# One layout for two batches of x, and a first q in two pieces: attention into an FFN on one core

## The chip, the core and the metric

One core of a Trainium2 chip runs the whole program. The metric is the device time of one execution in microseconds (us). The kernel before took 543.62 us, the median of 8 runs that lie between 543.4 and 544.74.

## The reference

Attention with a squared relu instead of a softmax, for 8 batches of 12 heads, 448 tokens and a head width of 64; then a block with a normalization and two FFN layers on x, which has 448 tokens of 768 features.

```python
scores = scale * np.matmul(q, k.transpose(0, 1, 3, 2))
attn = np.maximum(scores, 0.0) ** 2 / S
x = np.matmul(attn, v)            # heads side by side: (8, 448, 768)
mu, var = mean and variance of x over its 768 features
xn = (x - mu) / np.sqrt(var + 1e-06) * g_ln
out = x + np.maximum(xn @ w_ch1, 0.0) @ w_ch2    # 768 -> 3072 -> 768
```

Inputs and output are fp32; the kernel computes in bf16 with fp32 sums.

## The kernel before

TensorE does everything that is a product. Per batch the 12 heads go in three groups (n counts them over all batches, `NPER = 3` per batch). For a group: q and k are turned (line 474 on TensorE for batches 0 and 1, a DMA transpose at line 405 for the others), `att_QK` makes scores for seven blocks s of 64 tokens (line 552), ACT or DVE applies the relu (561, 563), DVE, POOL or ACT squares (578, 576), and `att_AV` multiplies by v (616). Its result is x transposed: features on partitions, tokens along the row, six blocks `ki` of 128 features.

`att_AV` copies it out of PSUM (helper at 354 for ACT and 356 for DVE) into `xT_e` or `xT_o`, for even and odd batches, each three blocks of 128 tokens, and `xT_left`, which holds the remaining 64 tokens of an even and an odd batch side by side. So a copy has two parts, `reg` (384 tokens) and `left` (64). From there three things are made:

- the mean over features: for batch 0 `mean_part` (681, 683) multiplies by a matrix of 1/768; for later batches POOL adds first (`sum_part`, 706 to 709) and `center` (785, 789) multiplies the sum;
- the centred x: DVE subtracts the mean (826 and 829 for batches 0 and 1, 807 for others), then ACT, or DVE, multiplies by the gain (814, 816). This is the input of FFN layer 1 (876 for the first three columns of batch 0, 893 for the rest; evacuated with a relu at 909 and 911);
- x token by token, from which variance and residual come: `after_x` turns it by a DMA transpose that SP issues (729 for the three blocks, 741 for the left one), DVE takes the statistics (754 to 756), ACT and DVE make the reciprocal root (765, 767). FFN layer 2 (950) needs these only when its result is evacuated (964).

`load_first` brings the first group of batch 0 as fp32 by SP's queue (344) and has it cast (356); all other loads go by POOL's queue, which casts on the way (324, 376, 416, 422, 392), at most eight in flight.

The order of the instructions is made by a planner, `Order`, before anything runs. Each piece of work has an estimated cost; `R.add` puts it among those that wait, with the engines that may do it, and `best` takes the one that can start first, on the engine that would finish it first. TensorE's work is put in by `R.pe` in an order of its own: for batch 0 whichever of two streams (scores, and the rest) can start sooner, afterwards by `greedy` and `segment`. Every engine then runs its own list strictly in that order, and waits at an instruction until its inputs are there. The planner's times only set the order. A few lines of the loop for batch 0:

```python
qk_stream += [("T", NPER)] + qks(NPER, 0, 3)
...
tA, tQ = (start_of(piece_deps(*st[0])) if st else FAR for st in (av_stream, qk_stream))
...
st = av_stream if tA <= tQ + 50.0 else qk_stream
```

Of the kernel before, what the change touches and what calls it, by code (L numbers as in the profile page):

```python
# [40 lines left out]
class Order:  # L41

    LAT = {"PE": 240.0, "ACT": 90.0, "DVE": 90.0, "POOL": 90.0, "SP": 0.0}
# [105 lines left out]
    def pe(self, cost, emit, deps=(), mode="F"):  # L151

        if mode != self.mode:
            cost += 90.0
        self.mode = mode
        op = Op("PE", cost, emit, deps, 0.0)
        while True:
            r = self.ready(op)
            p = self.best()
            if r is not None:  # L160
                t0 = max(r, self.free["PE"])
                if p is None or p[3] > t0:
                    break
            assert p is not None, "no work left that could release TensorE"
            self.wait.remove(p[1])
            self.commit(p[1], p[2], p[3])
        self.commit(op, "PE", t0)
        return op
# [28 lines left out]
def kernel(  # L197
# [43 lines left out]
    x_pool = ctx.enter_context(tc.tile_pool(name="x", bufs=2))  # L241
    xh_pool = ctx.enter_context(tc.tile_pool(name="xh", bufs=1))
# [16 lines left out]
    xT_e = const_pool.tile([P, 3, K1, P], bf16)  # L259
    xT_o = const_pool.tile([P, 3, K1, P], bf16)  # L260
    xT_left = const_pool.tile([P, K1, P], bf16)
# [8 lines left out]

    def xT_of(b):

        t, off = (xT_e, T) if b % 2 == 0 else (xT_o, 0)
        return t, xT_left[:, :, off:off + T]
# [3 lines left out]
    stage, vt, qkT, xT, xc, xm, mvs, rstd = {}, {}, {}, {}, {}, {}, {}, {}  # L278
# [49 lines left out]
    FIRST = ((0, 0, J), (1, 0, 3), (1, 3, J))  # L328

    def load_first():  # L330
# [3 lines left out]
        for i, (t, j0, j1) in enumerate(FIRST):  # L334
# [10 lines left out]
            ld = R.add("SP", 480.0, emit, [], key=float(i), load=(2 * P, (75.0, 43.0, 110.0)[i]))  # L345
# [119 lines left out]
    def att_T(n, part=0):  # L465
# [17 lines left out]
        if b == 0:  # L483
            evs = ops.setdefault(("T", n), [])
            pieces = list(enumerate(FIRST if n == 0 else ((0, 0, J), (1, 0, J))))
            for i, (t, j0, j1) in pieces[2 * part:2 * part + 2]:
# [37 lines left out]
    def qk_dep(n, s):  # L524
        b, pn = divmod(n, NPER)
        if ("T", n) in ops:
            if n == 0 and s >= FIRST[1][2]:
                return ops["T", n] if len(ops["T", n]) > 2 else None
            return ops["T", n][:2]
        if ("turn", b, 0) in ops:  # L530
            return [ops["turn", b, 0], ops["turn", b, 1]]
        return None

    def att_QK(n, s):
# [29 lines left out]
        late = FAR if n == 0 and s < FIRST[1][2] else 0.0 if s == 1 and n >= 2 * NPER else 600.0  # L564
# [35 lines left out]
    def att_AV(n, s):  # L600
# [24 lines left out]
        t, t_left = xT_of(b)  # L625

        free = ops.get(("x_read", b - 2), []) + ops.get(("turn_x", b - 2), [])
        if b % 2 == 0:
            free = free + ops.get(("turn_x", b - 1), [])
        evs = []  # L630
        if b == 0:
            for half in range(2):
                def evac(eng, half=half):
                    ki = pn + half * NPER
                    copy(eng, t[:, 0:3, ki, :], av_st[n][half][:, reg(b)].rearrange("p (m c) -> p m c", c=P))
                    copy(eng, t_left[:, ki, :], av_st[n][half][:, left(b)])
                ev = R.add(("DVE", "ACT"), (770.0, 760.0), evac, [op], key=-1.0)
                f_use(ev)
                evs.append(ev)
        else:  # L640
            def evac(eng, rest):
                ps = av_st[n, 1]
                if rest:
                    copy(eng, t_left[:, pn::NPER, :], ps[:, :, left(b)])
                else:
                    copy(eng, t[:, 0:3, pn::NPER, :].rearrange("p m h c -> p h m c"),
                         ps[:, :, reg(b)].rearrange("p h (m c) -> p h m c", c=P))
            ev0 = R.add(("DVE", "ACT"), (960.0, 800.0), lambda eng: evac(eng, False), [op] + free, key=-1.0)
            ev = R.add(("DVE", "ACT"), (295.0, 270.0), lambda eng: evac(eng, True), [op, ev0], key=-1.0)
            slot_use(ev)  # L650
            evs = [ev0, ev]
# [15 lines left out]
    def mean_part(n):  # L667
# [4 lines left out]
        def emit(eng):  # L672
# [5 lines left out]
            t, t_left = xT_of(b)  # L678
            for ki in (pn, pn + NPER):
                first, last = ki == 0, ki == K1 - 1  # L680
                nc.tensor.matmul(mean_ps[b][:, reg(b)], ones, t[:, 0:3, ki, :], start=first, stop=last,  # L681
                                 skip_group_check=True)
                nc.tensor.matmul(mean_ps[b][:, left(b)], ones, t_left[:, ki, :], start=False, stop=last,
                                 skip_group_check=True)
# [8 lines left out]
    def sum_part(n):  # L693

        b, pn = divmod(n, NPER)
        t, t_left = xT_of(b)

        def add(eng, rest):
            if rest:
                x0, x1 = t_left[:, pn, :], t_left[:, pn + NPER, :]  # L700
                s0, r_t = sum_t[:, left(b)], rsum_t[:, left(b)]
            else:
                x0, x1 = t[:, 0:3, pn, :], t[:, 0:3, pn + NPER, :]
                s0, r_t = (a[:, reg(b)].rearrange("p (m c) -> p m c", c=P) for a in (sum_t, rsum_t))
            if pn == 0:
                nc.gpsimd.tensor_add(s0, x0, x1)  # L706
            else:
                nc.gpsimd.tensor_add(s0, s0, x0)  # L708
                nc.gpsimd.tensor_add(s0 if pn < SUMMED[b] - 1 else r_t, s0, x1)
        k = 1 if pn == 0 else 2  # L710
        free = ops["x_read", b - 1] if pn == 0 else [ops["sum", n - 1]]
        a0 = R.add("POOL", 900.0 * k, lambda eng: add(eng, False), ops["x", n] + free, key=-2.0, port=True)
        ops["sum", n] = R.add("POOL", 250.0 * k, lambda eng: add(eng, True), [a0], key=-2.0,
                              port=True)
# [3 lines left out]
    def after_x(b):  # L718
# [4 lines left out]
        m0 = 0 if even else 4  # L723

        def turn(eng):
            a = x_pool.tile([P, 3, d_model], bf16, tag="x")
            for i in range(3):
                xm[u, m0 + i] = a[:, i, :]
            nc.sync.dma_start_transpose(
                a.rearrange("p m (k c) -> p (m k) c", c=P),  # L730
                xT_of(b)[0].rearrange("p m k c -> p (m k c)"))
        late = [ops["w1", K2 - 1]] if b == 0 else []
        tr = R.add("SP", 100.0, turn, xs + late + [ops.get(("f2_out", b - 2))], key=0.0, load=(3 * K1 * P, 18.0))

        deps_of = {m0 + i: tr for i in range(3)}
        ops["turn_x", b] = [tr]
        if not even:
            def turn_left(eng):
                a = xh_pool.tile([P, d_model], bf16, tag="xl")
                xm[u, 3] = a  # L740
                nc.sync.dma_start_transpose(
                    a.rearrange("p (k c) -> p k c", c=P), xT_left.rearrange("p k c -> p (k c)"))
            deps_of[3] = R.add("SP", 100.0, turn_left, xs + [ops.get(("m3_out", u - 1))],
                               key=0.0, load=(K1 * P, 18.0))
            ops["turn_x", b].append(deps_of[3])
        for m in sorted(deps_of):
            def stats(eng, m=m):
                if m == min(deps_of):
# [9 lines left out]
            if m == min(deps_of):  # L758
                ops["st0", b] = sto
            ops["st", u, m] = sto  # L760
        n_m = 3 if even else 4
        s0 = 0 if even else 3
# [3 lines left out]
        sq = R.add("ACT", 300.0, root, [ops["st", u, s0 + i] for i in range(n_m)], key=3.0)  # L766
# [6 lines left out]
    def center(b):  # L773

        st = {}
        t, t_left = xT_of(b)
        if b == 0:
            op = ops["mean", b]
        else:
            n_s = SUMMED[b]  # L780

            def emit(eng):
# [4 lines left out]
                for ki in rest:  # L787
                    for cols, i in ((reg(b), t[:, 0:3, ki, :]), (left(b), t_left[:, ki, :])):
                        nc.tensor.matmul(ps[:, cols], ones, i, start=False, stop=ki == rest[-1],
                                         skip_group_check=True)  # L790
# [29 lines left out]
        if b < 2:  # L820
            for ki in [pn + NPER * h for pn in range(NPER) for h in range(2)]:
                def sub_k(eng, ki=ki):
                    if ki == 0:
                        alloc()
                    mean = mean_ps[b]
                    nc.vector.tensor_sub(
                        xc[b][:, ki, reg(b)].rearrange("p (m c) -> p m c", c=P), t[:, 0:3, ki, :],
                        mean[:, reg(b)].rearrange("p (m c) -> p m c", c=P))
                    nc.vector.tensor_sub(xc[b][:, ki, left(b)], t_left[:, ki, :], mean[:, left(b)])
                s1 = R.add("DVE", 675.0, sub_k, [op], key=-2.0)  # L830
                subs.append(s1)
                c_ops.append(R.add(*GAIN_ON, lambda eng, ki=ki: gain(eng, ki), [s1], key=-2.5, port=True))
        else:
            for m in range(4):
# [25 lines left out]
    def ffn_1_first(b):  # L860
# [3 lines left out]
        def fill(eng):  # L864
# [5 lines left out]
            for i in range(N_FILL):  # L870
                nc.tensor.matmul(st[i % 2][0][:, :3 * P], ones, xT_e[:, :, 0, :], start=True, stop=True)
# [120 lines left out]
    def piece_deps(kind, n, *s):  # L992
# [3 lines left out]
        if kind == "T" and s:  # L996
            return [ops["qk_ld", 0, 0][2]]
# [152 lines left out]
    with tc.manual_schedule():  # L1150
# [28 lines left out]
        qk_stream += [("T", NPER)] + qks(NPER, 0, 3)  # L1179
# [20 lines left out]
        qk = [p for p in qk if p in qk_stream or p not in [("T", NPER)] + qks(NPER, 0, 3)]  # L1200
# [51 lines left out]
```

## Time and profile before

| | |
|---|---|
| median of 8 runs | 543.62 us |
| the profiled execution, its own time | 543.69 us |
| its span in the profile | 541.7 us |
| TensorE (PE) busy | 527.5 us, 97% |
| DVE, ACT, POOL busy | 286.2, 229.2, 113.5 us |
| chain that ended last, share of PE | 94% |
| first matmul, first FFN matmul | 5.01, 29.97 us |

The span is what the profiler recorded from the first to the last instruction; what lies around it is 2.0 us here. Busy is the time in which an engine had an instruction under way; TensorE's matmuls overlap, so a busy TensorE need not be at its peak. "Waits" are put down to what came last before an engine went on. In the chain each step is followed back to what released it. Durations of one instruction include its latency: two that follow each other on DVE or ACT overlap by some 0.08 to 0.1 us.

### The profile page before, as it was taken

Reading aid. Unit: us, or ns where it says so; the run is one execution under the profiler, and the core shown is the slowest. Engines: PE = TensorE matmul, PEld = TensorE weight load, DVE = VectorE, ACT = ScalarE, POOL = GpSimd, SP = SyncE. Lnnn points to the kernel's source line nnn. Section 1 sums busy time; section 2 is a strip of 40 time slices with the busy share of each in tenths; the row PEclk is TensorE's granted clock in tenths of the full one; section 3 lists DMA queues with packets and bytes.
Section 4 is the critical chain, followed back from the end, with each engine's and each line's share of the span. In section 5 each row is a group of like instructions: output and inputs, shape, how many; then the busy total and the mean of one; then the engine's idle time right before and its main releaser. Section 6 shows DMA issues by size and latency. Waiting matters only on the chain.

```text
span 541.7 us, 9897 instructions
## 1 busy us (share of the span) xinstructions
PE 527.5 (97%) x4208; PEld 285.7 (53%) x4208; DVE 286.2 (53%) x503; ACT 229.2 (42%) x380; POOL 113.5 (21%) x132
## 2 busy tenths in 40 slices
PE   4899999999999999999999999999999999999996
PEld 3444455555554455545555455555555545555553
DVE  5979557337774566735366446752556534530011
ACT  5977612124335642556125653265413654134200
POOL 6411700121350124311061121610220102100000
PEclk9999999999999999999999999999999999999999
DMA  9999999997299005970199502990032100510022
GB/s 195 205 198 185 209 162 169 155 137 136 69 157 181 7 1 94 194 114 2 31 108 204 75 1 55 161 187 1 1 68 66 30 0 1 111 36 1 1 58 60
DMA packets 141112, 51.83 MB, mean 96 GB/s; under 512 B 120966, under 2 KB 136844, under 8 KB 141068
## 3 DMA queue, kind: packets, MB, share of 16 engines
q0 software_dynamic: 81072, 25.50, 43.2%
q1 hardware_dynamic: 55516, 14.88, 18.4%
q10 hardware_dynamic: 4480, 10.82, 7.2%
q8 instruction: 33, 0.54, 0.4%
q14 instruction: 11, 0.09, 0.1%
HBM read 51.91 MB, written 11.01 MB: 116 GB/s over the span
## 4 chain that ended last, share of the span: by engine, by line
PE 94%; DVE 2%; DMA 1%; ACT 1%; issue 0%; POOL 0%; POOLq 0%; ACTq 0%; DVEq 0%
PE o_ps L950 41%; PE ps L893 40%; PE sc L552 6%; PE ps L616 5%; DMA t<-in_k_dram 1%; DVE a L578 1%; PE ps L876 1%; ACT a L561 1%; PE ps L474 0%; DVE t L356 0%; PE slot L785 0%; PE ps L681 0%; DVE a L563 0%; ACT a L576 0%; POOL t L324 0%
## 5 line engine op out<-in xcount | busy, mean ns | idle before, releaser
L893 PE MATMUL ps<-a,w 128*128 128x448 bf16 x1134 | 220.4, 353 | 0.0
L950 PE MATMUL o_ps<-w,h 128*128 128x384 bf16 x1200 | 199.7, 326 | 0.0
L893 PEld LDWEIGHTS <-w 128*128 128x128 bf16 x1134 | 108.3, 98 | 108.3 <-issue 10.8
L950 PEld LDWEIGHTS <-h 128*128 128x128 bf16 x1200 | 116.1, 98 | 81.5 <-issue 5.5
L909 ACT ACTIVATE h<-ps 128x448 bf16<-128x448 f32 (+1 forms) x162 | 85.5, 528 | 104.3 <-PE ps L893 103.3
L561 ACT ACTIVATE a<-sc 128x896 bf16<-128x896 f32 x102 | 90.4, 921 | 85.5 <-PE sc L552 81.2
L563 DVE TENSOR_SCALAR a<-sc 128x896 bf16<-128x896 f32 x57 | 62.0, 1087 | 103.4 <-PE sc L552 103.2
L578 DVE TENSOR_TENSOR a<-a 128x896 bf16<-128x896 bf16 x158 | 99.5, 667 | 3.4 <-ACT a L561 3.3
L964 DVE SCALAR_TENSOR_TENSOR o_t<-o_ps,r_t,a 128x384 f32<-128x384 f32 x56 | 34.4, 615 | 107.2 <-PE o_ps L950 106.8
L552 PE MATMUL sc<-t 64*64 64x448 bf16 x672 | 47.8, 361 | 2.0 <-ACT a L561 1.3
L616 PE MATMUL ps<-a,v_t 64*64 64x448 bf16 x636 | 37.0, 351 | 1.5 <-DVE a L578 0.5
L814 ACT ACTIVATE a<-a,g_sb 128x448 bf16<-128x448 bf16 x39 | 23.0, 657 | 26.0 <-DVE a L807 24.9
L552 PEld LDWEIGHTS <-t 64*64 64x64 bf16 x672 | 17.5, 106 | 23.6 <-issue 18.2
L616 PEld LDWEIGHTS <-v_t 64*64 64x64 bf16 x672 | 20.2, 107 | 16.8 <-issue 5.7
L392 POOL DMA_DIRECT2D t<-in_q_dram x12 | 19.3, 1773 | 27.2 <-DMA t<-t 25.7
L708 POOL TENSOR_TENSOR sum_t<-sum_t,xT_o 128x384 f32<-128x384 f32 x7 | 6.4, 914 | 85.4 <-ACT xT_o L354 72.3
L950 PE MATMUL o_ps<-w,t 128*128 128x384 bf16 x144 | 23.9, 326 | 0.0
L392 POOL DMA_DIRECT2D t<-in_k_dram x12 | 23.7, 2527 | 0.0
L708 POOL TENSOR_TENSOR sum_t<-sum_t,xT_e 128x384 f32<-128x384 f32 x6 | 5.5, 913 | 81.1 <-ACT xT_e L354 75.6
L376 POOL DMA_DIRECT2D v_t<-in_v_dram x16 | 17.9, 1495 | 15.0 <-DMA w<-in_moe_w_ch_dram 7.2
L706 POOL TENSOR_TENSOR sum_t<-xT_o 128x384 f32<-128x384 bf16 x4 | 3.6, 910 | 80.1 <-DVE a L578 66.0
L950 PEld LDWEIGHTS <-t 128*128 128x128 bf16 x144 | 13.9, 98 | 9.8 <-issue 0.7
(73 smaller groups left out, 235.2 us busy)
## 6 DMA issues: line engine op xcount, KB each, us to landing
out_dram<-o_t ACTq DMA_DIRECT2D x54, 192.0 KB, 3.1
v_t<-in_v_dram POOLq DMA_DIRECT2D x16, 336.0 KB, 15.2
w<-in_moe_w_ch_dram POOLq DMA_DIRECT2D x4, 1152.0 KB, 39.9
t<-in_q_dram POOLq DMA_DIRECT2D x12, 336.0 KB, 7.3
t<-in_k_dram POOLq DMA_DIRECT2D x12, 336.0 KB, 10.3
w<-in_moe_w_ch_dram POOLq DMA_DIRECT2D x4, 768.0 KB, 16.3
w<-in_moe_w_ch_dram POOLq DMA_DIRECT2D x1, 1536.0 KB, 30.2
t<-in_q_dram POOLq DMA_DIRECT2D x5, 224.0 KB, 9.9
```

What stands on the lines that cost most here:

```text
L376: nc.gpsimd.dma_start(vt[b][half * T:(half + 1) * T], v[b, half * 6:half * 6 + 6].rearrange("h (p j) d -> p h (j d)", j=J))
L392: nc.gpsimd.dma_start(stage[b][half * T:(half + 1) * T, t].rearrange("p j (h d) -> p j h d", d=D), src[b, half * 6:half * 6 + 6].rearrange ...
L552: nc.tensor.matmul(sc[rows_of(half), r, :S], qkT[b][rows_of(r), 1, s * NPER + pn, rows_of(half)], qT[:, :, pn, rows_of(half)], start=True, ...
L561: nc.scalar.activation(attn[n, s], st[0][:, :, :S], Act.Relu, scale=rc2)
L563: nc.vector.tensor_scalar(attn[n, s], st[0][:, :, :S], rc2, 0.0, op0=Alu.mult, op1=Alu.max)
L578: nc.vector.tensor_mul(attn[n, s], attn[n, s], attn[n, s])
L616: nc.tensor.matmul(av_st[n][half][rows_of(hh)], vt[b][rows_of(half), 2 * pn + hh, s * D:(s + 1) * D], attn[n, s][rows_of(half), hh, :], st ...
L814: nc.scalar.mul(o, o, g_sb[:, ki:ki + 1])
L893: nc.tensor.matmul(st[0], w1[:, ki, ni * P:(ni + 1) * P], xc[b][:, ki, :], start=(i == 0), stop=(i == K1 - 1))
L909: nc.scalar.activation(o, st[0][:, c], Act.Relu)
L950: nc.tensor.matmul(o_st["ps"], stat(ki), w2[:, ki, j * hd:(j + 1) * hd], start=(ki == 0), stop=(ki == K2 - 1))
L964: nc.vector.scalar_tensor_tensor(o_st[u, m][:, j * hd:(j + 1) * hd], ps, rstd[b][:, ri:ri + 1], xm[u, m][:, j * hd:(j + 1) * hd], op0=Alu. ...
```

## The change

For batches 0 and 1 x is no longer kept in three pieces. One tile `xT_all` holds, for each of the six feature blocks, the 896 tokens of batch 1 and batch 0 side by side; the copies out of PSUM, the subtractions, mean matmuls and POOL's sums then have one part of 448 instead of 384 and 64. The transposes of these two batches go feature block by feature block: six DMAs of three token blocks for batch 0 and six of four for batch 1, in place of one and two. Later batches keep the layout of before, in the same tile. x token by token lives in one tile `x_all` of seven blocks instead of two pools. The first q is loaded, cast and turned in two pieces (token blocks 0 to 3 and 4 to 6), as k was already, and copied in two. In the planner a matmul that starts before 12.4 us is taken to cost 1.85 times as much, and one block of batch 1's scores, not three, may be put ahead of the first FFN matmuls. The lines of before stand 7 to 19 lines further down in the new file.

```diff
+    COLD = 12400.0
...
+        if t0 < self.COLD:
+            op.cost = cost = 1.85 * cost
         self.commit(op, "PE", t0)
...
-    xT_e = const_pool.tile([P, 3, K1, P], bf16)
-    xT_o = const_pool.tile([P, 3, K1, P], bf16)
-    xT_left = const_pool.tile([P, K1, P], bf16)
+    xT_all = const_pool.tile([P, J * d_model], bf16)
+    x_all = const_pool.tile([P, J, d_model], bf16)
...
+    x0_T = xT_all.rearrange("p (k c) -> p k c", c=2 * S)
...
+        if b < 2:
+            return x0_T[:, :, (1 - b) * S:(2 - b) * S]
+        t = xT_all.rearrange("p (m k c) -> p m k c", k=K1, c=P)
+        off = T if b % 2 == 0 else 0
+        return t[:, 0:3] if b % 2 == 0 else t[:, 4:7], t[:, 3, :, off:off + T]
...
-    FIRST = ((0, 0, J), (1, 0, 3), (1, 3, J))
+    FIRST = ((0, 0, 4), (0, 4, J), (1, 0, 3), (1, 3, J))
...
-            ld = R.add("SP", 480.0, emit, [], key=float(i), load=(2 * P, (75.0, 43.0, 110.0)[i]))
+            ld = R.add("SP", 480.0, emit, [], key=float(i), load=(2 * P, (40.0, 35.0, 43.0, 110.0)[i]))
...
-                    copy(eng, t[:, 0:3, ki, :], av_st[n][half][:, reg(b)].rearrange("p (m c) -> p m c", c=P))
-                    copy(eng, t_left[:, ki, :], av_st[n][half][:, left(b)])
-                ev = R.add(("DVE", "ACT"), (770.0, 760.0), evac, [op], key=-1.0)
+                    copy(eng, xT_of(b)[:, ki, :], av_st[n][half])
+                ev = R.add(("DVE", "ACT"), (620.0, 560.0), evac, [op], key=-1.0)
...
-                nc.tensor.matmul(mean_ps[b][:, reg(b)], ones, t[:, 0:3, ki, :], start=first, stop=last,
-                                 skip_group_check=True)
-                nc.tensor.matmul(mean_ps[b][:, left(b)], ones, t_left[:, ki, :], start=False, stop=last,
+                nc.tensor.matmul(mean_ps[b], ones, xT_of(b)[:, ki, :], start=ki == 0, stop=ki == K1 - 1,
                                  skip_group_check=True)
...
+        def turn(ms, tiles, deps):
+
+            a, z = tiles
+            for k in range(K1 if u == 0 else 1):
+                def emit(eng, k=k):
+                    if u == 0:
+                        o = x_all[:, a:z, k * P:(k + 1) * P]
+                        i = x0_T[:, k, a * P:z * P]
+                    else:
+                        o = x_all[:, a:z].rearrange("p m (k c) -> p (m k) c", c=P)
+                        i = xT_all[:, a * d_model:z * d_model]
+                    nc.sync.dma_start_transpose(o, i)
+                tr = R.add("SP", 100.0, emit, deps, key=0.0, load=((z - a) * K1 * P / (K1 if u == 0 else 1), 18.0))
+                ops["turn_x", b].append(tr)
...
-                    nc.vector.tensor_sub(
-                        xc[b][:, ki, reg(b)].rearrange("p (m c) -> p m c", c=P), t[:, 0:3, ki, :],
-                        mean[:, reg(b)].rearrange("p (m c) -> p m c", c=P))
-                    nc.vector.tensor_sub(xc[b][:, ki, left(b)], t_left[:, ki, :], mean[:, left(b)])
-                s1 = R.add("DVE", 675.0, sub_k, [op], key=-2.0)
+                    nc.vector.tensor_sub(xc[b][:, ki, :], xT_of(b)[:, ki, :], mean_ps[b])
+                s1 = R.add("DVE", 560.0, sub_k, [op], key=-2.0)
...
-        qk_stream += [("T", NPER)] + qks(NPER, 0, 3)
+        qk_stream += [("T", NPER)] + qks(NPER, 0, 1)
```

## The prediction

> **What bounds the kernel now.** I read the page first, then the waits of TensorE, then five-microsecond windows over the start, then the chain and the timeline there. The waits of TensorE:
>
> ```profile
> PE ps L474 <- DVE t L356: 5.0, 1, 5.0
> PE sc L552 <- ACT a L561: 1.3, 3, 0.6
> PE sc L552 <- ACT t L354: 0.6, 1, 0.6
> PE ps L616 <- DVE a L578: 0.5, 3, 0.2
> ```
>
> All of them lie before the first FFN matmul. The windows (length, then busy time of PE, PEld, DVE, ACT, POOL, each with its count):
>
> ```profile
> 5.00:10.00 5.00, 4.13 (x117) 3.30 (x119) 2.58 (x6) 2.98 (x4) 3.21 (x6) 1.00 1.26 204
> 10.00:15.00 5.00, 3.68 (x79) 2.15 (x73) 4.89 (x9) 4.49 (x7) 2.73 (x5) 1.00 1.27 204
> 15.00:20.00 5.00, 4.32 (x108) 2.53 (x100) 5.00 (x12) 4.80 (x8) 2.12 (x3) 1.00 1.25 206
> 20.00:25.00 5.00, 4.24 (x104) 2.21 (x100) 5.00 (x11) 5.00 (x8) 2.56 (x4) 1.00 1.26 204
> 25.00:30.00 5.00, 4.20 (x38) 2.04 (x35) 3.65 (x10) 3.49 (x8) 1.54 (x2) 1.00 1.25 206
> 30.00:35.00 5.00, 5.00 (x32) 2.28 (x32) 4.49 (x12) 3.99 (x7) 1.64 (x2) 1.00 1.24 191
> ```
>
> From 30 us TensorE is full in every window I asked for. Its idle time is 541.7 - 527.5 = 14.2 us: 9.4 before 30 us, and the last 4.8 after its last matmul (505.73 + 31.21 = 536.94). So two things can move the end: the time at which the first FFN matmul starts (29.97 us), and a stall put into the full stretch. Before 30 us DVE and ACT are full, and DMA carries 204 GB/s. The chain over that stretch (start, length, what):
>
> ```profile
> 2.43 7.19 DMA t<-in_k_dram
> 9.66 0.56 PE ps L474 x24
> 10.33 0.62 DVE t L356
> 10.95 2.14 DVE a L578 x4
> 25.15 0.96 ACT a L576
> 26.15 0.38 PE ps L616 x4
> 29.97 3.62 PE ps L876 x18
> ```
>
> It waits for the second k group of batch 0 at 9.62, then passes from DVE to ACT and back.
>
> [...] The mean matmuls start at 27.81, 27.98 and 28.00: the pair takes 0.19. [...] the subtraction takes 546 ns for 384 elements and 210 for 64, so about 143 ns is fixed. [...] ACT's relu of 896 takes 921. [...] the transpose of 18 blocks holds SP's queue for 9.14 us at 27.25, beside the weights, and 2.66 us at its quickest.
>
> **The change, part by part.** *Mean matmuls.* Batch 0 has six pairs, batch 1's tail two; eight matmuls of 64 columns go, [...]
>
> *Copies of x, batch 0.* On DVE the pair starts at 16.15 and the next instruction at 16.75: 0.60. One of 448 out of PSUM takes 619 ns (row of the FFN relu on DVE); consecutive DVE instructions overlap by 0.08 (four squares in 2.22 at 0.61 each, a pitch of 0.535), so 0.54: 0.06 saved, three times. On ACT the pair costs 0.48 (15.62 to 16.10) and one of 448 some 0.43.
>
> *Subtractions.* The pairs start 0.60 apart (28.47, 29.07, 29.67); one of 448 some 0.535. On the path only the first counts, -0.065: afterwards the gain (pitch 0.60 on ACT) and three FFN matmuls (0.60) set the pace.
>
> *First q in two pieces.* q lands at 0.74 + 3.6 = 4.34 and TensorE starts at 5.01. Half as a first piece I put at 3.85, so TensorE starts near 4.3. But scores need all of q, and k's first piece, now third in the queue, at about 5.0 (4.88 before: 1.28 + 3.6). DVE then casts k to 5.38 and copies three pieces (0.35 + 0.27 + 0.27, q's second ready near 5.86): first scores at 6.53 against 6.86, and the first relu on ACT at 7.17 against 7.50. After three relus ACT is free at 9.63. The next group's k still lands at 9.62, so its transposes end at 10.3 as before. The gain of 0.33 ends in that wait.
>
> *What the planner then does.* In the changed program's order ACT takes one 896 copy of each later transposed q/k group (three in all), one relu and the only ACT square move to DVE. The group's copy starts on ACT at 10.33; from there to the end of the last relu of batch 0 ACT has 15 relus (pitch 0.82: six took 5.07, the last 0.92), that copy and one more [...], and two x copies: 10.33 + 12.30 + 1.60 + 0.86 = 25.09. I followed the waits beside it and found ACT never idle. Before, from 10.54: 16 relus 13.12, two x pairs 0.94, the square 0.96, sum 25.56, and the trace ends at 26.10: 0.5 us of waits. The changed kernel saves this, but its last square is on DVE. ACT's last three relus give their results at 23.55, 24.37 and 25.19 (25.09 and 0.1 of latency, each 0.82 apart). DVE, never idle by then, squares the first from 23.97, the second from 24.51 to 25.05, then in its order stands the copy of batch 1's first q (to 25.58), and only then the third, whose result is there at 26.20. Last attention matmuls 26.25 against 26.15: **+0.10**. The rest of the way (three mean pairs, the gain's copy, the last mean pair) has the same length; the subtraction gives back 0.065. First FFN matmul at about 30.0: **+0.04**.
>
> *Early scores of batch 1, one for three.* The trace shows one group of four at 27.49 ahead of the FFN, and the changed order has one there too: nothing. If DVE or ACT were free earlier the old form could have put two more there; they are not.
>
> *Transposes, 12 pieces for 3.* SP issues 6 of 3 blocks and 6 of 4. A small one cost 1.24 for 6 blocks and 2.66 for 18, so 0.53 + 0.12 per block: 6 x 0.89 + 6 x 1.01 = 11.4 us of SP against 2.66 + 2.66 + 1.24 = 6.6, unloaded, hidden since nothing but batch 2's turn at 86.75 is queued behind. The first now waits only for its own copy and leaves at about 16 us, between loads. The blocks are as many as before. They are read by the statistics on DVE. Batch 0's began at 86.36 and in the changed order stand five relus of 1.137 earlier, near 80; their transposes landed at 27.25 + 25.1 = 52.4. Batch 1's began at 93.17 and now stand near 91; they landed at 73.63 + 11.2 = 84.8. Cover: 6 us. Were it gone, DVE's next FFN relu would wait behind, and TensorE after two PSUM banks, from about 92 on, microsecond for microsecond.
>
> *Sums on POOL* (448 for 384 + 64) and *batch 1's copies*: hidden, DVE and ACT have 0.5 to 1.3 us free in each 5 us there, POOL more. The order of TensorE after the first FFN matmul has the same counts and the same 100 changes between attention and FFN; batch 1's mean comes one FFN group (1.2 us) earlier, beside a copy of 0.9 us that just fits.
>
> Sum: +0.04 on the profiled run's 543.69 (span 541.7, 2.0 around it), which stands 0.07 above the median of the runs, 543.62. Prediction **543.7**.
>
> **Rivals.** *B, faster:* ACT's 0.5 us of waits go, and the four 0.06 savings on each engine chain instead of hiding; if also DVE's last copy and square don't queue (0.5) and the k group lands 0.2 sooner, the first FFN matmul comes 1.3 us earlier: 542.3. For it: both engines are full there. Against: each hands to the other. *C, slower:* the k group lands later. One more load goes ahead of it [...]. ACT has no slack behind 10.33, so a delay passes one to one; if 256 more packets [...] cost 1.2 us (the first q took 3.6 to land), 544.9. It decides from 1.1 us on. *A, slower:* the pieces of batch 1 transpose no faster each than a block did at 27 us, 25.1 / 18 = 1.4 us: 24 from 62 end at 95.5, 3.5 us past the point of 92: 547.2. Against: all of this ended by 84.8 before, with 16 of 24 blocks now left at 62. *That the split does nothing* is inside the forecast.
>
> **How the numbers follow.** The measurement tells 0.2%, 1.09 us, from no change. Forecast (within it) 0.64, range of its own 543.0 to 544.4 (the copies on ACT may be 0.70 or 1.0 each: -0.2 to +0.4, and waits of up to 0.5 that I missed); B 0.15; C 0.12; A 0.09. Faster 0.15, same 0.64, slower 0.21. Low 542.5 and high 545.3 take in half of B, C, and leave out A.
>
> **What would show it.** First scores near 6.5; the copy on ACT at 10.3; ACT without gaps to 25; a first FFN matmul between 29.5 and 30.5; no TensorE wait after it. A TensorE wait at 60 to 64 or 88 to 98, or a k group landing away from 9.6, would make it wrong.

## The result and the profile after

The changed kernel takes 545.49 us (median of 10 runs, 545.05 to 545.97) against 543.55 for the one before (543.4 to 544.74 over 28 runs beside it): ratio 1.0034, 95% interval 1.0026 to 1.0042. It is slower by 1.94 us, and outside the predicted range of 542.5 to 545.3. The profiled execution took 545.47, with a span of 543.7.

The waits of TensorE in the first 36 us, changed kernel:

```profile
PE ps L483 <- DVE t L365: 7.2, 3, 4.1
PE sc L561 <- ACT a L570: 1.0, 3, 0.4
PE ps L625 <- DVE a L587: 0.7, 1, 0.7
```

The first of these stood at 5.0 in one wait. It is now 7.2 in three: TensorE waits for the cast of q, and then twice for casts of k. The chain of work in that stretch (start, length, what):

```profile
1.77 0.47 SPq L353
2.28 7.84 DMA f<-in_k_dram
10.15 0.44 DVE t L365
10.63 2.02 PE ps L483 x67
...
32.43 3.66 PE ps L887 x18
```

Before, the chain came in at 2.43 with a load of the second k group and the first FFN matmul stood at 29.97. Now it comes in with SP's fourth load, the second piece of the *first* k, which lands at 10.12; the FFN starts at 32.43, 2.46 later. DVE's instructions show both pieces:

```profile
3.61 1.04 DVE L365 CAST t<-f 128x512 bf16<-128x512 f32 x2 [2.58 <-DMA f<-in_q_dram]
7.62 0.36 DVE L365 CAST t<-f 128x384 bf16<-128x384 f32 x1 [2.96 <-DMA f<-in_k_dram]
10.15 0.43 DVE L365 CAST t<-f 128x512 bf16<-128x512 f32 x1 [1.19 <-DMA f<-in_k_dram]
```

The same in the kernel before, where the first line holds the cast of q and that of k's first piece:

```profile
4.33 1.03 DVE L356 CAST t<-f 128x896 bf16<-128x896 f32 x2 [3.29 <-DMA f<-in_q_dram]
6.55 0.42 DVE L356 CAST t<-f 128x512 bf16<-128x512 f32 x1
```

The two pieces of q are early, as the change wants: their casts start at 3.61, where the cast of the whole q started at 4.33. But k, whose pieces were cast right behind q and at 6.55 before, comes at 7.62 and 10.15. In the windows (length, then PE, PEld, DVE, ACT, POOL) DVE and ACT have 1.31 and 0.35 us of work in the second five microseconds, where they had 2.58 and 2.98:

```profile
5.00:10.00 5.00, 1.75 (x34) 0.87 (x28) 1.31 (x4) 0.35 (x1) 3.12 (x5) 1.00 1.18 221
10.00:15.00 5.00, 4.72 (x105) 3.97 (x104) 4.51 (x8) 4.39 (x6) 2.38 (x4) 1.00 1.27 205
```

After 35 us TensorE never waits, in either kernel. So the balance of the spans has three terms. The FFN starts 2.46 later. From there to TensorE's last matmul it is 507.24 for 506.97, +0.27. From that matmul to the end it is 4.03 for 4.76, -0.73. Together +2.00, which is the difference of the spans.

**Why k is late.** The traffic of the first load queues, microsecond by microsecond: packets, megabytes, share of the engines. q1 is SP's queue, q0 POOL's. The kernel before, from 4 to 5 us (first pair) and from 5 to 6 us (second pair):

```profile
q1 hardware_dynamic: 365, 0.32, 96.5%
q0 software_dynamic: 22, 0.02, 12.0%
...
q0 software_dynamic: 193, 0.17, 109.5%
q1 hardware_dynamic: 56, 0.04, 15.1%
```

The changed kernel, in the same two microseconds:

```profile
q1 hardware_dynamic: 46, 0.04, 28.4%
q0 software_dynamic: 24, 0.02, 27.0%
...
q0 software_dynamic: 125, 0.11, 68.6%
q1 hardware_dynamic: 130, 0.10, 41.7%
```

These counts hold more than data: each load closes with records of 4 bytes, 16 for a load of q or k. By their sizes, 35 of k's 512 data packets are left at 5 us in the kernel before, and 447 in the changed one. Two things lie behind this.

The larger comes first. In the changed kernel all packets of q have started by 3.6 us, earlier than before. But from 3.6 to 5 us SP's queue starts 74 packets, where it had 534 in the kernel before, and POOL's has 26 there; single packets are then under way for up to 1.4 us. POOL's first packet comes at 3.80, when SP's queue has already slowed. Had SP's queue gone on as in the kernel before, nearly all of k would have been through by 5 us (an estimate from the 534). Why it nearly stops isn't shown.

From 5 us on POOL's loads are in full flow and the two queues go side by side, 130 packets of SP's to 125 of POOL's, then 156 to 125 and 116 to 137. A packet of POOL's is under way for 88 ns (0.686 x 16 / 125 us), one of SP's for 51 (0.417 x 16 / 130). So SP's queue gets a good third of the time that the packets of both took from 5 to 6 us (41.7 of 110.3%), and its last packets of k come between 9 and 10. What decides which queue's packet goes next isn't shown.

### The profile page after: what moved, and what is told of

Its sections match the earlier page's. It is cut to its first block, busy times and chain, and to the rows that moved or that the text cites. A ratio compares the mean times of both kernels' runs of the same rounds, so it can differ in the third digit from the quotient of the medians.

```text
span 543.7 us, 9861 instructions
## 1 busy us (share of the span) xinstructions
PE 529.1 (97%) x4200; PEld 286.4 (53%) x4200; DVE 285.1 (52%) x488; ACT 230.0 (42%) x376; POOL 112.6 (21%) x129
## 4 chain that ended last, share of the span: by engine, by line
PE 95%; DVE 3%; DMA 1%; SPq 0%; ACT 0%; issue 0%; DVEq 0%
PE o_ps L961 41%; PE ps L904 40%; PE sc L561 6%; PE ps L625 6%; DVE a L587 1%; DMA f<-in_k_dram 1%; PE ps L483 1%; PE ps L887 1%; DVE a L572 1%; DVE t L365 0%; SPq L353 0%; PE ps L691 0%; PE slot L800 0%; DVE xT_all L365 0%; ACT a L828 0%; DVE a L839 0%
## 5 line engine op out<-in xcount | busy, mean ns | idle before, releaser
L975 DVE SCALAR_TENSOR_TENSOR o_t<-o_ps,r_t,x_all 128x384 f32<-128x384 f32 x56 | 34.4, 615 | 108.2 <-PE o_ps L961 108.0
L720 POOL TENSOR_TENSOR sum_t<-sum_t,xT_all 128x384 f32<-128x384 f32 (+2 forms) x25 | 19.5, 779 | 168.0 <-ACT xT_all L363 148.3
L718 POOL TENSOR_TENSOR sum_t<-xT_all 128x384 f32<-128x384 bf16 (+2 forms) x13 | 9.9, 763 | 129.0 <-DVE a L587 97.2
L363 ACT CAST xT_all<-ps 128x768 bf16<-128x768 f32 (+3 forms) x38 | 21.5, 567 | 23.8 <-DVE xT_all L365 13.2
L561 PEld LDWEIGHTS <-t 64*64 64x64 bf16 x672 | 17.9, 107 | 23.4 <-issue 17.9
L821 DVE TENSOR_TENSOR a<-xT_all,sum_t 128x768 bf16<-128x768 bf16 (+1 forms) x24 | 19.4, 852 | 6.7 <-ACT sum_t L813 6.5
```

Source lines behind the costliest of these rows:

```text
L363: nc.scalar.copy(o, i)
L561: nc.tensor.matmul(sc[rows_of(half), r, :S], qkT[b][rows_of(r), 1, s * NPER + pn, rows_of(half)], qT[:, :, pn, rows_of(half)], start=True, ...
L975: nc.vector.scalar_tensor_tensor(o_st[u, m][:, j * hd:(j + 1) * hd], ps, rstd[b][:, ri:ri + 1], xm[u, m][:, j * hd:(j + 1) * hd], op0=Alu. ...
```

## The experiments

The theories were these. Theory 1 in its first form (1a): one more load on SP costs half a microsecond of its issue, and k then falls behind the start of POOL's loads. In its second form (1b): the smaller and more numerous packets of the pieces cost the time. The rival (2): the new layout, or what the planner makes of it, costs it.

### Splitting nothing but q's load, by columns

```diff
-                nc.sync.dma_start(raw[0][:, t, :, cols], rows[:, 0::NPER, cols])
+                for c in ((slice(0, 4 * D), slice(4 * D, J * D)) if i == 0 else (cols,)):
+                    nc.sync.dma_start(raw[0][:, t, :, c], rows[:, 0::NPER, c])
```

In the kernel before; q is still cast whole.

> The kernel before, with nothing changed but that the load of the first q is two DMAs by columns (256 packets of 1024 bytes and 256 of 768, for 256 of 1792); the cast waits for both. Theory 1, either form: k's first piece lands near 7.6 (4.9 before), its second near 10 (6.3 before), time +1.7 to +2.5, 545.2 to 546.0. Theory 2: no change, 543.4 to 543.8.

545.94 us, ratio 1.0045 (1.003 to 1.006). DVE's instructions:

```profile
8.07 0.36 DVE L357 CAST t<-f 128x384 bf16<-128x384 f32 x1 [3.15 <-DMA f<-in_k_dram]
10.02 0.43 DVE L357 CAST t<-f 128x512 bf16<-128x512 f32 x1 [1.05 <-DMA f<-in_k_dram]
```

This one edit brings k to 8.07 and 10.02 and the first FFN matmul to 32.57: all of the loss, with the old layout and the old planner.

### The same by rows, with no more packets than before

```diff
+                for r in ((slice(0, 1), slice(1, 2)) if i == 0 else (slice(0, 2),)):
+                    nc.sync.dma_start(raw[0][:, t, r, cols], rows[:, 0::NPER, cols][:, r])
```

> The kernel before, with the load of the first q as two DMAs by rows: 128 packets of 1792 bytes each, so as many packets as before and of the same size, but one more issue of about 0.5 us ahead of k. Theory 1a (it is the half microsecond of issue): k's pieces land late as with columns, time +1.7 to +2.5. Theory 1b (it is the 256 more and smaller packets): k's pieces at 4.9 and 6.3, time 543.4 to 543.9. Theory 2: no change.

545.45 us, ratio 1.0033 (1.002 to 1.0046); k's casts at 7.14 and 9.39, the FFN at 31.73. Two DMAs of 128 packets of 1792 bytes make k nearly as late as two of 256 smaller ones. The number of DMAs does most of it. Whether the smaller packets add the other 0.5 us (545.94 - 545.45) isn't shown, since the two intervals overlap.

### A small load ahead of k

The 3 KB of gains, issued by SP second instead of last.

```diff
                 nc.sync.dma_start(raw[0][:, t, :, cols], rows[:, 0::NPER, cols])
+                if i == 0:
+                    nc.sync.dma_start(g_rows, moe_g_ln.rearrange("(ko kp) -> ko kp", kp=P))
...
-            nc.sync.dma_start(g_rows, moe_g_ln.rearrange("(ko kp) -> ko kp", kp=P))
+            pass
```

> The kernel before, with the load of the gains (6 rows of 512 bytes) issued second on SP's queue instead of fourth: k's pieces are issued some 0.45 us later, with next to no data ahead of them and q whole. Theory 1a: k's first piece lands late (between 5.5 and 7.6), its second at 8 or later, time +1 to +2.5. Theory 1b and theory 2: 543.4 to 544.0.

545.14 us, ratio 1.0032 (1.002 to 1.0044). The chain at the start:

```profile
2.13 6.62 DMA f<-in_k_dram
...
31.23 3.61 PE ps L878 x18
```

Six packets ahead of k are no traffic to speak of; what they take is 0.4 us of SP's issue. k's first piece still came in time (the first scores at 6.83), against the expectation; its second was cast at 8.78 instead of 6.55, and the kernel lost 1.6 us. So it is not the bytes ahead of k that decide. It is the later issue, or the later place in SP's queue; these two go together in every run here.

### k from ACT's queue

```diff
-    nc.scalar.activation(warm, eps_sb, Act.Sqrt)
...
-                nc.sync.dma_start(raw[0][:, t, :, cols], rows[:, 0::NPER, cols])
+                (nc.scalar if t else nc.sync).dma_start(raw[0][:, t, :, cols], rows[:, 0::NPER, cols])
+                if i == len(FIRST) - 1:
+                    nc.scalar.activation(warm, eps_sb, Act.Sqrt)
```

ACT issues k's pieces at 0.74 and about 1.2, beside SP's q; its table load of 1.28 us and the first activation, at 0.73 and 2.03 before, move behind them, to 1.81 and 3.11. First in the changed kernel:

> The changed kernel, with both k pieces issued from ACT's queue at 0.74 and 1.2 (ACT's table load behind them), so that nothing waits for a third and fourth slot of SP. Theory 1a (late issue puts k behind POOL's loads): k's first piece lands by 4.9 and its second by 6.0; first FFN matmul 29.5 to 31; time 543.4 to 544.5. If more packets or the split itself were the cause: k still at 7 or later, 545 to 546.

543.65 us, ratio 0.9997 (0.9989 to 1.0006): 1.84 us better than the changed kernel, with q still in two pieces.

```profile
5.36 0.70 DVE L366 CAST t<-f 128x384 bf16<-128x384 f32 x2 [0.63 <-DMA f<-in_q_dram]
7.22 0.42 DVE L366 CAST t<-f 128x512 bf16<-128x512 f32 x1
```

Now k waits for q: DVE's idle time ends with q's second piece. The same in the kernel before, with q whole:

> The kernel before, with both k pieces issued from ACT's queue. Theory 1a: k's first piece lands by 4.7, k's second by 5.8 (6.3 before), clear of most of POOL's loads; since the next group of k lands at 9.6 and sets the pace, time 543.0 to 543.6, perhaps a little under the kernel before.

544.00 us, ratio 1.0007 (0.9998 to 1.0016). The gain that I expected isn't there. q itself took 4.19 us instead of 3.6 (its cast starts at 4.96 for 4.33), with k now under way beside it. From 3 to 5 us all queues together moved 0.73 MB, as much as in the kernel before: here the second queue added an issuer, and no bandwidth.

### POOL's loads later

Four fills of a spare tile ahead of POOL's first work, in the changed kernel; POOL's first load is issued at 2.22 instead of 1.44.

```diff
+        for _ in range(4):
+            nc.gpsimd.memset(pad, 0.0)
         make_identity(nc, identity)
```

> The changed kernel, with four small fills of an unused tile ahead of POOL's identity, so that POOL's first load is issued some 0.8 us later (2.2 for 1.44). If POOL's loads are what k meets: k's first piece lands by 5.5 (7.6 in the changed kernel) and its second by 8 (10.1), although SP issues them as late as before; the next k group lands 0.3 to 0.8 later than 9.6 + 1; time 544.0 to 545.0, under the changed kernel. If only SP's issue counts: k as late as in the changed kernel, time 545.5 to 546.3.

544.75 us, ratio 1.002 (1.0008 to 1.0032). k is cast at 6.86 and 8.83, 0.76 and 1.32 us earlier than in the changed kernel though later than I expected, and the FFN starts at 31.66: issuing POOL's loads 0.78 us later moves k. What POOL's issue does to SP's queue isn't plain. POOL's first packet comes only 0.3 us later (4.09 for 3.80), and SP's queue still slows at 3.6, but less: 196 packets from 3.6 to 5 us for 74. The delay doesn't give all back, because the loads that were delayed are now late themselves:

```profile
PE ps L625 <- DVE a L587: 0.7, 1, 0.7
PE ps L625 <- DMA v_t<-in_v_dram: 0.6, 1, 0.6
```

### The layout without the split

```diff
-    FIRST = ((0, 0, 4), (0, 4, J), (1, 0, 3), (1, 3, J))
+    FIRST = ((0, 0, J), (1, 0, 3), (1, 3, J))
...
-            ld = R.add("SP", 480.0, emit, [], key=float(i), load=(2 * P, (40.0, 35.0, 43.0, 110.0)[i]))
+            ld = R.add("SP", 480.0, emit, [], key=float(i), load=(2 * P, (75.0, 43.0, 110.0)[i]))
```

> The changed kernel with the first q loaded, cast and turned whole again (three pieces on SP's queue); the new layout, the planner's factor of 1.85 and the single early score block stay. Theory 1 (the fourth load on SP's queue puts both k pieces behind POOL's first loads): k's first piece lands near 4.9, its second near 6.3, as in the kernel before; first FFN matmul at 29.5 to 30.2; time 543.2 to 543.9. Rival theory 2 (the new layout, with its 12 transposes and its other planned order, is what costs): still 545.0 to 545.8, first FFN matmul near 32.

544.39 us, ratio 1.0031 (1.0012 to 1.0049), with runs from 543.66 to 547.6. k is in time (its second cast at 6.82), yet the kernel is slower than before, and the first FFN matmul stands at 31.10. What stands new among TensorE's waits:

```profile
PE ps L625 <- DVE t L365: 1.1, 2, 0.9
PE ps L625 <- DMA v_t<-in_v_dram: 0.6, 1, 0.6
```

In this order TensorE's first product with v stands at 11.15, ahead of scores, where before it came at 12.50; v lands at 12.27. That order comes from the planner's factor of 1.85. Without the factor too:

```diff
-        if t0 < self.COLD:
-            op.cost = cost = 1.85 * cost
```

> As whole_q, and the planner's factor of 1.85 for early matmuls is taken out too: what is left of the change is the layout of x for two batches (and one early score block for three). If the planner's new order made up the remainder of 0.3% in whole_q (it puts the first multiplication by v ahead of scores, and v lands only at 12.3): first FFN matmul at 29.8 to 30.1, time 543.3 to 543.8. If the layout and its early transposes do: as whole_q, 544.0 to 544.8, first FFN matmul near 31.

**542.56 us**, ratio 0.9981 (0.9973 to 0.9989): faster than both kernels by more than the measurement's uncertainty, though by only 0.19% of the one before. The order at the start is again that of before, and the chain runs:

```profile
0.74 3.54 DMA f<-in_q_dram
...
29.70 3.56 PE ps L884 x18
```

### The factor with the split

The changed kernel with the last edit alone:

> The changed kernel without the planner's factor of 1.85; its loads stay as they are. With q whole the factor cost 1.8 us. If it costs the same wherever k lands: 543.5 to 544.0, first FFN matmul near 31.0. If the factor was harmful only because AV was put ahead of v's landing while k was early, and here k's late landing sets the start in any order: 545.1 to 545.8, first FFN matmul 32.2 to 32.6. If the factor is what keeps TensorE fed while k is late: 546.0 or more.

544.90 us, ratio 1.0026 (1.0018 to 1.0033). Each of the three forecasts missed; it lies between the first two. The four kernels with the new layout make a table:

| us | without the factor | with it |
|---|---|---|
| q whole | 542.56 | 544.39 |
| q in two pieces | 544.90 | 545.49 |

The split costs 2.34 us without the factor and 1.10 with it; the factor costs 1.83 with q whole and 0.59 with the split. The 1.10 and the 1.83 are good to about 1 us, by the interval of the run with q whole and the factor, and the intervals of the two runs behind the 0.59 overlap. From before to after, in this order: -0.99 for the layout with one early block of scores for three (the two were not taken apart), +2.34 for the split, +0.59 for the factor, in sum +1.94.

### Where the layout's 1 us comes from

Between the profiles of before and of the layout alone the first FFN matmul moves from 29.97 to 29.70, and the FFN stretch from 506.97 to 506.91. The largest term is the end: 4.76 us from the last matmul to the end become 4.09. The last store lands 2.05 us behind DVE's last instruction in both. Behind that, in the records of SP, the kernel before has a gap among its last bookkeeping instructions, 0.49 us from the start of one to the start of the next. With one more DMA on SP the gap stands one instruction earlier, with two fewer two later. In the kernels with the new layout, whose SP list is longer by nine or ten DMAs, there is none. If the length of SP's list is the cause, nine loads that nothing reads should do the same:

```diff
+            for i in range(9 if b == 2 else 0):
+                nc.sync.dma_start(spare[:, i, :], moe_g_ln.rearrange("(o c) -> o c", o=48)[i:i + 1, :])
```

> The kernel before, with nine loads of 64 bytes each, which nothing reads, added on SP's queue behind the first DMA transpose of batch 2's x (after 80 us), so that SP's list is longer by nine DMAs, about as in the changed kernel. Theory (the tail): in the profile of before SP stands still for 0.49 us among its last instructions, after the last store has landed, at a place that moves with the number of DMAs on SP; with a longer list it falls where SP waits anyway. Then the time from TensorE's last matmul to the end goes from 4.75 to 4.0 to 4.2 us, and the median from 543.55 to 542.9 to 543.1, with the first FFN matmul unchanged at 29.9 to 30.1. Rival (the shorter tail of the changed kernel comes from its layout): 4.6 to 4.8 us of tail and 543.4 to 543.8.

543.20 us against 543.61 beside it, ratio 0.9991 (0.9982 to 0.9999): -0.41 us, a little less than forecast, and the profile's end is 4.1 us. A gap of 0.49 us is still there, but it now lies ahead of the landing of the last store, where SP waits anyway. So nine loads that nothing reads give the shorter end without the new layout. In the layout's own gain the end is the larger part, 0.67 of 0.99 us. What SP does in the gap the records don't say. An 8192-byte packet on one of the queues that the profile calls "instruction" (q14) is recorded in the last microseconds of every run with the old layout (at 541.36 in the kernel before) and of none with the new one. Whether the gap hangs on it isn't shown.

### Is it the lateness of k, or TensorE's slow stretch?

In the changed kernel four scores take 0.58 us on TensorE until about 14.5 us, and 0.38 afterwards; before, ten take 0.73 at 10.12 and four 0.38 at 11.51. The slow rate is half the quick one: at the slow rate twelve scores take 1.33, eight more for 0.75 us, and at the quick rate 0.76, eight more for 0.38. (Differences are taken because matmuls overlap: the first 18 of the FFN take 351 ns each on average and 3.6 us together.) The traces record the granted clock itself, at full speed from 9.31 in the kernel before and only from 14.89 in the changed one. (Ahead of that they have no record, and the windows print 1.00.) Before, TensorE's longest gap between its first matmul at 5.01 and that point is 0.57 us; in the changed kernel it waits 2.79 us for k ahead of 8.03. So the full clock came 5.58 us later where k was late; that the gaps are the cause these two traces don't show. For this question there are two more kernels like the changed one, in which plain copies stand for the DMA transposes, so that the turning of x and of q and k of batches 2 to 7 is left out. One of them got matmuls that nothing reads:

```diff
-                    nc.sync.dma_start_transpose(o, i)
+                    nc.sync.dma_start(o, i.rearrange("p (j c) -> p j c", c=P))
...
+    warm_ps = ps_s.tile([P, 2, 512], fp32, tag="s")
+    for _ in range(27):
+        nc.tensor.matmul(warm_ps[:, 0, :P], ones, ones, start=True, stop=True, skip_group_check=True)
...
+                    if n == 0 and i == 2:
+                        for _ in range(32):
+                            nc.tensor.matmul(warm_ps[:, 0, :P], ones, ones, start=True, stop=True, skip_group_check=True)
```

> The changed kernel with its DMA transposes replaced by plain DMA copies of the same blocks: q and k of batches 2 to 7 and x token by token are left unturned, which leaves that part of the computation out. The first of them leaves at about 18 us, so the start stays the changed kernel's: k's casts at 7.4 to 7.8 and 9.7 to 10.3, four scores still in 0.58 us until about 14 us, first FFN matmul 32.0 to 32.7. It is the partner of the run with added matmuls; its own time, 544.5 to 546, says nothing else.

> The same (plain copies in place of the DMA transposes, so that part left out) with matmuls of 128 columns on a constant added that nothing reads: 27 at TensorE's start, before q is there, and 32 between the transposes of q and those of the late k. In the changed kernel's trace TensorE's matmuls are slow (four scores in 0.58 us) until 14.6 us, in the one of before until 9.6 us (then 0.38). Theory: a part of the 2.46 us by which the first FFN matmul is late is this slow stretch, which follows from TensorE standing without work while k is under way; with TensorE kept busy four scores take 0.38 from about 9 us on, and against its partner the first FFN matmul comes 0.4 to 1.1 us earlier and the median is as much lower, with k's casts where they were. Rival: DVE and ACT set the pace between 10 and 32 us, the slow matmuls hide behind them, and all of the loss is k's lateness: within 0.2 us of its partner in both.

545.04 us (544.7 to 546.04) for the partner and 545.12 (544.86 to 546.53) with the added matmuls: no difference, as the rival said. But the edit did only half of what it should. TensorE's instructions with the added matmuls, in an execution that was the slowest of the ten and has k later than its partner, at 8.70 and 11.34:

```profile
9.97 0.76 PE L567 MATMUL sc<-t 64*64 64x448 bf16 x12 [0.48 <-DVE t L368]
11.82 2.02 PE L486 MATMUL ps<-identity,t 64*64 64x64 bf16 x68 [1.08 <-DVE t L368]
13.61 0.58 PE L567 MATMUL sc<-t 64*64 64x448 bf16 x2
```

The first scores are quick (12 in 0.76, for 1.33), but after waits of 2.14 and 1.08 us for k TensorE is slow again at 11.82. The recorded clock is full from 4.53, behind the first 27 added matmuls (1.09 to 4.15), half from 11.35 to 14.77, and full again; the partner's scores are quick only from 14.70 (8 in 0.57). From the end of the added matmuls at 6.97 to the fall TensorE had 1.14 us of work (0.38 from 9.11 and 0.76 from 9.97), so the stretch ahead of this fall was not empty.

A share of the slow stretch in the loss is thus not excluded. What the profiles say for k's lateness: from the start of the second k cast to the first FFN matmul it is 22.28 us in the changed kernel, 22.55 with q split by columns, 22.34 by rows, 22.45 with the gains ahead, 22.83 with POOL later, 22.58 and 22.23 in this pair, and 21.66 in the changed kernel without the factor. Where that cast comes at 6.52 to 7.23 it is 23.2 to 23.4, and 24.28 with q whole and the factor (cast at 6.82); there other waits take over. So when k is late, the start of the FFN follows it closely.

One execution shows what the clock can cost. In the profile of the kernel with nine more loads k is cast at 8.00, and the way to the FFN is 23.41. The full clock is on record there only from 16.73; with the gains ahead, in nearly the same program, it is from 14.18. In the chain the products with v take 1.87 us at 13.44 (20 matmuls) as against 0.99 (18, at 14.21), and that is nearly all of the difference between 23.41 and 22.45. In the changed kernel without the factor the clock is full from 11.85, against 14.89 with it, and with q whole from 9.67, against 11.45; so some of what is put down to the factor may be the clock's. None of this is taken apart.

## Why the prediction was wrong

**First q in two pieces: the step that failed.** The pieces of q came as put (casts at 3.61 and right behind it). "k's first piece, now third in the queue, at about 5.0" failed: cast at 7.62, and the second at 10.15, of which the step said nothing. Even at the rate it used (3.6 from issue to landing) the issue at 1.77 gave 5.4. And this rate did not hold: the piece took 5.8 us from issue to landing, and the second 7.8, because SP's queue nearly stopped from 3.6 to 5 us and then went side by side with POOL's loads, 130 packets to 125 from 5 to 6 us. Why it stopped is open; that a later k meets POOL's loads could have been read. POOL's first loads, issued at 1.44 and 2.43, stood in the trace of before, as did their first packets at 4.6 us and the 35 packets of k that were left after 5 us: the second half of k had finished just ahead of them. A half-microsecond delay there was never priced. First scores stood at 9.01, not 6.53.

**"The gain of 0.33 ends in that wait"** fell with it: the wait for the second k group no longer set anything, since the first k came later. (That group itself landed at 10.5, for 9.62.)

**Rival C** came nearest in mechanism, "one more load goes ahead of it", and had the wrong transfer: not the second k group on POOL's queue but the first k behind the split on SP's own. Its 544.9 was 0.6 short, and its 1.2 us for 256 more packets was an estimate of mine; that 544.9 lay near is luck, since the second k group, on which it rested, was 0.9 us late but not waited for.

**What the planner then does.** Forecast +0.10. The factor costs 0.59 in the changed kernel and 1.83 with q whole. I had followed DVE and ACT through the new order, but not when v lands, on which TensorE's new order ran with q whole. The 1.60 us for ACT's two copies of 896 was an estimate of mine; in the changed kernel the next instruction starts 0.81 and 0.80 us behind such a copy (12.79 to 13.60, 18.95 to 19.75).

**Copies and subtractions.** Each size held: the copy in one part lies 0.53 apart from its successor on DVE, as against 0.60 for the pair. That TensorE gains nothing from the mean matmuls holds too: those of 448 start 0.19 apart (29.41, 29.60, 29.79), as the pairs did. The layout alone brought the FFN 0.27 us earlier, more than the 0.065 put on the path. What else the layout gains, 0.7 us at the end, no step looked for.

**Transposes, sums, rival A.** They cost nothing on the path. TensorE is full in every ten microseconds from 55 to 105, and the first statistics start at 83.2. (The small transposes took 1.18 us at the quickest, for the 0.89 and 1.01 put down. Why the transpose of 18 blocks held SP's queue longer beside the weights, 9.14 us for 2.66 at its quickest, the traces don't show.) **Rival B** asked for a gain from the layout and the order; the layout alone gave 542.56, near its 542.3, but by other terms, so this too is luck.

## What to carry to other kernels

At a kernel's start, price a split load by the issue that it adds, not by its bytes alone: write down when each queue's first packet moves, and how many packets of the critical transfer are still to come at that moment. Here those that were left moved at 116 to 156 a microsecond, where the queue nearly alone had moved 365. A load that lands "in time" in the trace may have done so by half a microsecond. Before calling a layout faster, look at the last four microseconds too: part of a gain can come from the end of a bookkeeping queue and be had without the layout.

## What the hardware showed that I had not expected

- SP issued one load per 0.5 us (0.74, 1.28, 1.77, 2.28 here), with little regard to its size: 0.4 us for 3 KB, 0.48 for 448 KB. Here one more issue of 0.4 us cost 1.6 us of the kernel's time.
- From 4 to 5 us all engines together moved 70 packets (46 and 24) in the changed kernel, after 309 from 3 to 4 us. The drop begins at 3.6, ahead of POOL's first packet at 3.80; why stays open. All seven profiles with q in two loads ahead of k on SP's queue show such a drop: 100 to 224 packets on all queues from 3.6 to 5 us, for 556 in the kernel before. The two with k on ACT's queue don't (540 and 639).
- Executions of one kernel differ in when k lands. In one execution of the kernel with nine more loads, 544.55 us long where the median is 543.20, 11 data packets of k stayed behind from 6 to 8 us, k's second cast came at 8.00 for 6.55, and the FFN started at 31.41.
